# Sign of a converted weight set by a two-slope scaling on ScalarE instead of a second bit operation on VectorE, for 56 of the 68 weight pieces

## The chip, the cores and the metric

One Trainium2 chip; the kernel runs on one of its cores. The metric is the device time of one execution in microseconds (us). The engines are named as the profile names them: PE (TensorE matmul) and PEld (its weight load), DVE (VectorE), ACT (ScalarE), POOL (GpSimd), SP (SyncE).

## The reference, cut to what matters

A linear attention with exponential features, then two feed-forward layers:

```
q_p, k_p = phi(q * scale), phi(k * scale)      # exp(x @ omega.T - row maximum)
kv = einsum('bhsm,bhsd->bhmd', k_p, v)
x  = einsum('bhsm,bhmd->bhsd', q_p, kv) / den  # 2304 tokens x 512
xn = x / rms(x) * rms_g
y  = (silu(xn @ w_gate) * (xn @ w_val)) @ w_out        # hidden 1536
h  = y @ w_in
out = (h * cos(h)) @ w_out2                            # hidden 2048
```

The activations are float32, the five weight matrices reach the kernel as float64. The kernel has to turn each weight into float32 from its two 32-bit words before PE can use it, and it does so by arithmetic on their bits.

## The kernel before, in words

**Stages.** In the first stage (to about 311 us) PE works off 36 tiles of keys and queries (projection L392, transposes L410 and L468, sums L553 and L430) and, mixed into the later query tiles, the products of the first group of four of the twelve hidden columns of layer 1 (`product` L789, `out1` L854). The second stage (311 to about 586 us) does the other eight columns of layer 1 by seven products of half-size blocks (L1053, L1132). The third does layer 2 (L789 `h_ps`, L781 to L783 `o_ps`).

**The weights.** They are cut into 68 pieces of 128x512 values: 36 of layer 1 (for each of 12 columns f a gate piece e=0, a value piece e=1 and an output piece e=2) and 32 of layer 2 (16 columns, e=0 and 1). `Weights.todo` is their order: the twelve of the first group as gate, value, output of each column (so pieces 2, 5, 8 and 11 are output pieces), then for each of two groups of four columns the eight gate and value pieces and after them the four output pieces (20 to 23 and 32 to 35), then layer 2 (36 to 67).

**The conversion of one piece** is `exponent` and `front`:

- ACT (L161): the high words, read as float32 at a stride of two, are multiplied by 2**-112. That moves the exponent into place and gives W, of which there is one buffer.
- DVE (L167): f = W shifted left by 3, which drops the sign.
- DVE (L169): f = (W and SIGN) or f, which puts the sign back.
- DVE (L171): sign and exponent of f are written over the high words in `raw`.
- DVE (L178): the low words times 2**-52 times that, into `raw`.
- POOL (L183): f + that, the float32 value. `split` then makes a rounded high part (ACT, L188) and the rest (POOL, L191); pieces after the twelfth first go to DRAM (`keep`) and come back (`ask`).

**What sets the order.** Every engine takes its instructions in the order in which the program writes them. `front` is a generator with a yield after nearly every instruction; `tick`, `pace` and `get` take one step of it at fixed places between the attention's and the layers' own instructions. So the conversion's DVE operations stand in one queue with the row maxima (L401), the quotients (L440 to L442), the norm (L458), the transposed copies (L420), the gating (L840, L842) and the halves of x (L482), and W of the next piece (L161) stands in ACT's queue between the exponentials (L403), which PE's next products wait for. The ACT operation of piece c+1 is written after L171 of piece c.

The functions that the change touches, and what calls them:

Of the kernel before, what the change touches and what calls it, by code (L numbers as in the profile page):

```python
# [38 lines left out]
AF = mybir.ActivationFunctionType  # L39
ALU = mybir.AluOpType  # L40
# [8 lines left out]
SIGN = -(1 << 31)  # L49
# [6 lines left out]
def attention_then_ffn(ctx: ExitStack, tc: tile.TileContext, qT, kT, v, omT, wc1, rms_g, wc2, out, B, H, S, D):  # L56
    nc = tc.nc
# [50 lines left out]
    def f32(ap):  # L108
        return ap.bitcast(F32)
# [11 lines left out]
    class Weights:  # L121
# [26 lines left out]
        def load(self, c, queue=None):  # L148
            queue = queue or (nc.scalar if self.early else nc.sync)
            if c < len(self.todo) and c not in self.loaded:  # L150
# [4 lines left out]
                queue.dma_start(a, src.bitcast(I32).rearrange("p (n two) -> p n two", two=2))  # L155
                self.raw[c] = a

        def exponent(self, c):
            if c in self.raw:
                w = conv.tile([P, 512], I32, tag="W", name=f"W{c}", bufs=1)  # L160
                nc.scalar.mul(f32(w), f32(self.raw[c][:, :, 1]), 2.0 ** -112)  # L161
                self.w[c] = w

        def front(self, c):
            w, raw = self.w.pop(c), self.raw.pop(c)
            f = conv.tile([P, 512], I32, tag="f", name=f"f{c}", bufs=3)
            nc.vector.tensor_scalar(f, w, 3, None, op0=ALU.logical_shift_left)  # L167
            yield
            nc.vector.scalar_tensor_tensor(f, w, SIGN, f, op0=ALU.bitwise_and, op1=ALU.bitwise_or)  # L169
            yield  # L170
            nc.vector.tensor_scalar(raw[:, :, 1], f, SIGN_AND_EXPONENT, None, op0=ALU.bitwise_and)  # L171
            if not self.early:
                self.load(c + 2)
            yield
            self.exponent(c + 1)
            yield
            rest = f32(raw[:, :, 1])
            nc.vector.scalar_tensor_tensor(rest, raw[:, :, 0].bitcast(U32), 2.0 ** -52, rest,  # L178
                                           op0=ALU.mult, op1=ALU.mult)
            if c - 1 in self.f and c > self.fused:  # L180
                self.keep(c - 1)
            yield
            nc.gpsimd.tensor_tensor(f32(f), f32(f), rest, op=ALU.add)  # L183
            self.f[c] = f32(f)
            yield
# [325 lines left out]
    with tc.manual_schedule():  # L511
# [362 lines left out]
        def h_cos(blk, f, h, r, front, rate):  # L874
            o = fp.tile([P, 2, NB], F32R, tag="t", name=f"o{blk}_{f}", bufs=3)
            nc.scalar.activation(r, r, AF.Sin, bias=half_pi)  # L876
            wts.pace(front / 4, rate / 2)
            nc.vector.tensor_tensor(r, h, r, op=ALU.mult)  # L878
            nc.scalar.copy(o[:, 0], r)  # L879
            wts.pace(front / 4, rate / 2)  # L880
            nc.vector.tensor_tensor(o[:, 1], r, f32(o[:, 0]), op=ALU.subtract)  # L881
            return o
# [338 lines left out]
        for n in range(N2 + 2):  # L1221
            rate, front = 0, wts.rate(len(wts.todo) + 1, 52 - n)
            if n < N2:
                g = steps2[n][0]
                if n == starts[g] + 3:
                    wts.freed = base if g == 0 else done_at[g - 1]
                if g + 1 < len(GROUPS2) and n >= starts[g] + 3:
                    rate = rate_of(done_at[g + 1], starts[g + 1] - n - 8)
            if 2 <= n <= N2:
                hid[N1 + n - 1] = h_cos(*steps2[n - 1][1:3], *hid[N1 + n - 1], front, rate / 2)  # L1230
            flush(3)
            if due:
                unit()
                unit()
            for m in [n] if 0 < n < N2 - 3 else [n, n + 1] if n == N2 - 3 else [n + 1] if n == N2 - 2 else []:
                hid[N1 + m] = hidden(*steps2[m][1:3])
            if n >= 2:
                g0, b0, f0, st, en = steps2[n - 2]
                out2(g0, b0, f0, hid.pop(N1 + n - 2), st, en)
            if n in fetches:  # L1240
                fetch(fetches[n], f"yhl{steps2[n][0]}_{fetches[n]}")
            flush(3)
            if due:
                unit()
                unit()
            wts.pace(front / 2, rate / 2)
# [47 lines left out]
```

## Time and profile before

| | |
|---|---|
| three timed runs | 1000.8, 998.75, 999.22 us; median 999.22 |
| the profiled execution | 998.17 us, of which 996.4 us from the first instruction to the last |
| mean granted TensorE clock | 0.998 |
| PE, PEld | busy 977.5 us (98%), 922.8 us (93%) |
| DVE | busy 722.5 us (73%), 1251 instructions |
| ACT | busy 513.2 us (52%), 1117 instructions |
| POOL | busy 369.8 us (37%), 333 instructions |

PE's busy time is an average over three stages with different limits, so the table alone does not tell where PE waits; that is read from stretches. Busy times of PE come from modelled ends, and a busy PE can still be slower than its best. The chain of waits is the chain of work that ended last, followed back from the last instruction; "issue" in it is time in which an engine waited for nothing that the profile shows.

### The profile page before, as it was taken

To read this page: it belongs to the slowest core of one execution; us is meant where nothing else is said; L and a number is where in the kernel's file an instruction comes from. 1 tells how busy PE (TensorE), PEld (TensorE's weight loads), DVE (VectorE), ACT (ScalarE), POOL (GpSimd) and SP (SyncE) were. 2 spreads that over 40 slices of the span, in tenths; PEclk is the share of its full clock that TensorE was granted. 3 is DMA by queue.
4 is the path that set the end of the run, shared out by engine and by line. 5 is a ranking of instruction groups with operands and counts; after the bars stand their busy time and mean duration, and the time that the engine had idled before them with its cause. 6 is when DMAs were issued, how large, how long until landed. Compare 5 with 4: busy or idle time off the path is not lost.

```text
span 996.4 us, 16203 instructions
## 1 busy us (share of the span) xinstructions
PE 977.5 (98%) x5905; PEld 922.8 (93%) x5905; DVE 722.5 (73%) x1251; ACT 513.2 (52%) x1117; POOL 369.8 (37%) x333
## 2 busy tenths in 40 slices
PE   8999999998999999999999998999999999999998
PEld 7988998998999999999999997999999999999997
DVE  6797789988983558599776788776667776666655
ACT  6777775775533524346353545554444444434443
POOL 2133348747945866277433662111103310000000
PEclk9999999999999999999999999999999999999999
DMA  8555176785779788757978976443134442004201
GB/s 298 152 168 191 58 250 235 283 280 199 265 234 348 291 310 316 279 163 239 390 247 317 313 264 215 148 138 128 43 127 148 134 159 99 1 29 151 107 32 63
DMA packets 81438, 194.58 MB, mean 195 GB/s; under 512 B 8016, under 2 KB 38864, under 8 KB 81360
## 3 DMA queue, kind: packets, MB, share of 16 engines
q1 hardware_dynamic: 79920, 188.78, 54.2%
q10 hardware_dynamic: 1440, 4.78, 1.4%
q8 instruction: 46, 0.75, 0.3%
q14 instruction: 32, 0.26, 0.1%
HBM read 136.38 MB, written 57.15 MB: 194 GB/s over the span
## 4 chain that ended last, share of the span: by engine, by line
PE 84%; DVE 8%; issue 2%; ACT 2%; POOL 2%; ACTq 0%; DVEq 0%; POOLq 0%
PE h_ps L789 20%; PE X L1053 10%; PE y L1132 10%; PE Y L1053 8%; PE o_ps L783 7%; PE o_ps L782 7%; PE o_ps L781 6%; PE gv_ps L789 6%; PE y_ps L854 3%; PE kv_ps L553 2%; PE num_ps L430 2%; PE qp_ps L392 1%; DVE f L169 1%; PE kp_ps L392 1%; DVE f L167 1%
## 5 line engine op out<-in xcount | busy, mean ns | idle before, releaser
L789 PE MATMUL h_ps<-yhl,w 128*128 128x384 f32 x1152 | 217.2, 337 | 0.0
L789 PEld LDWEIGHTS h_ps<-yhl,w 128*128 128x128 f32 x1152 | 204.7, 188 | 8.1
L183 POOL TENSOR_TENSOR f<-f,raw 128x512 f32<-128x512 f32 x68 | 94.1, 1384 | 292.2 <-DVE raw L178 247.7
L191 POOL TENSOR_TENSOR w<-b,w 128x512 fp32r<-128x512 f32 x72 | 98.8, 1377 | 77.3 <-ACT w L188 67.7
L876 ACT ACTIVATE turns<-turns,half_pi 128x384 f32<-128x384 f32 x96 | 59.2, 617 | 110.4 <-DVE turns L871 110.4
L781 PE MATMUL o_ps<-w,o 128*128 128x512 f32 x288 | 112.1, 389 | 2.6 <-ACT o L879 2.6
L783 PE MATMUL o_ps<-w,o 128*128 128x512 f32 x288 | 114.0, 396 | 0.0
L782 PE MATMUL o_ps<-w,o 128*128 128x512 f32 x288 | 113.7, 395 | 0.0
L789 PE MATMUL gv_ps<-xhl,w 128*128 128x384 f32 x576 | 109.0, 337 | 1.8 <-DVE den L440 0.7
L789 PEld LDWEIGHTS gv_ps<-xhl,w 128*128 128x128 f32 x576 | 101.3, 189 | 3.2 <-issue 1.2
L1132 PE MATMUL y<-t,w 128*128 128x384 f32 x576 | 101.0, 334 | 0.0
L1132 PEld LDWEIGHTS y<-t,w 128*128 128x128 f32 x576 | 99.9, 188 | 0.0
L881 DVE TENSOR_TENSOR o<-turns,o 128x384 fp32r<-128x384 f32 x96 | 56.0, 583 | 50.0 <-ACT o L879 49.4
L879 ACT CAST o<-turns 128x384 fp32r<-128x384 f32 x96 | 49.3, 514 | 68.2 <-DVE turns L878 67.6
L878 DVE TENSOR_TENSOR turns<-h_ps,turns 128x384 f32<-128x384 f32 x96 | 53.4, 556 | 38.8 <-ACT turns L876 37.7
L1053 PE MATMUL X<-T,w 128*128 128x384 f32 x432 | 80.7, 334 | 0.0
L870 DVE SCALAR_TENSOR_TENSOR r<-turns,h_ps 128x384 f32<-128x384 int32 x96 | 53.1, 553 | 35.3 <-ACT turns L869 35.2
L1053 PEld LDWEIGHTS X<-T,w 128*128 128x128 f32 x432 | 75.4, 188 | 0.0
L869 ACT ACTIVATE turns<-h_ps,quarter 128x384 int32<-128x384 f32 x96 | 55.6, 580 | 32.2 <-PE h_ps L789 31.9
L783 PEld LDWEIGHTS o_ps<-w,o 128*128 128x128 f32 x288 | 54.0, 188 | 11.8 <-DVE o L881 0.3
L781 PEld LDWEIGHTS o_ps<-w,o 128*128 128x128 f32 x288 | 54.1, 188 | 11.6 <-ACT o L879 3.0
L169 DVE SCALAR_TENSOR_TENSOR f<-W,f 128x512 int32<-128x512 int32 x68 | 63.8, 939 | 1.0
(97 smaller groups left out, 1769.4 us busy)
## 6 DMA issues: line engine op xcount, KB each, us to landing
raw<-wc SPq DMA_DIRECT2D x59, 512.0 KB, 4.9
yhl<-yh_dram SPq DMA_DIRECT2D x32, 768.0 KB, 5.8
T<-T_dram SPq DMA_DIRECT2D x20, 768.0 KB, 9.2
kept<-f SPq DMA_DIRECT2D x56, 256.0 KB, 5.0
b<-kept SPq DMA_DIRECT2D x56, 256.0 KB, 4.1
B<-x_dram SPq DMA_DIRECT2D x15, 768.0 KB, 7.2
x_dram<-xhl SPq DMA_DIRECT2D x12, 768.0 KB, 5.8
s<-x_dram SPq DMA_DIRECT2D x24, 384.0 KB, 6.2
```

Source lines behind the costliest of these rows:

```text
L169: nc.vector.scalar_tensor_tensor(f, w, SIGN, f, op0=ALU.bitwise_and, op1=ALU.bitwise_or)
L183: nc.gpsimd.tensor_tensor(f32(f), f32(f), rest, op=ALU.add)
L191: nc.gpsimd.tensor_tensor(t[:, 1, to], src, f32(t[:, 0, to]), op=ALU.subtract)
L781: nc.tensor.matmul(o, w[0], x[0], start=first, stop=False)
L782: nc.tensor.matmul(o, w[0], x[1], start=False, stop=False)
L783: nc.tensor.matmul(o, w[1], x[0], start=False, stop=last)
L789: nc.tensor.matmul(o, w[i], x[j], start=n == 0, stop=n == len(terms) - 1)
L869: nc.scalar.activation(a, h, AF.Identity, bias=quarter, scale=1.0 / (2 * math.pi))
L876: nc.scalar.activation(r, r, AF.Sin, bias=half_pi)
L881: nc.vector.tensor_tensor(o[:, 1], r, f32(o[:, 0]), op=ALU.subtract)
L1053: nc.tensor.matmul(o, w[:, i, c + kk * P:c + (kk + 1) * P], x[:, j, kk], start=begin and n == 0, stop=n == 5, skip_group_check=True)
L1132: nc.tensor.matmul(acc[e], w[:, i, e * P:(e + 1) * P], t[:, j], start=f == fs[0] and i + j == 0, stop=f == fs[-1] and j == 1)
```

## The change: what it does

For 56 of the 68 pieces (all but the twelve output pieces of layer 1, which are layer 1, e=2) ACT's scaling becomes a parametric ReLU: a positive high word is multiplied by 2**-112 as before, a negative one by 2**-112 * 2**32. The exponent of a negative number so comes out larger by 32, and 32 in the exponent field is the bit that the shift by 3 moves into the sign's place. The DVE operation that put the sign back is not issued for these pieces; for the other twelve nothing changes.

```diff
+        def signed(self, c):
+            layer, f, e = self.todo[c]
+            return (layer, e) != (1, 2)
+
         def exponent(self, c):
             if c in self.raw:
                 w = conv.tile([P, 512], I32, tag="W", name=f"W{c}", bufs=1)
-                nc.scalar.mul(f32(w), f32(self.raw[c][:, :, 1]), 2.0 ** -112)
+                hi = f32(self.raw[c][:, :, 1])
+                if self.signed(c):
+                    nc.scalar.activation(f32(w), hi, AF.Prelu, scale=2.0 ** -112, alpha=2.0 ** 32)
+                else:
+                    nc.scalar.mul(f32(w), hi, 2.0 ** -112)
                 self.w[c] = w
...
             nc.vector.tensor_scalar(f, w, 3, None, op0=ALU.logical_shift_left)
             yield
-            nc.vector.scalar_tensor_tensor(f, w, SIGN, f, op0=ALU.bitwise_and, op1=ALU.bitwise_or)
+            if not self.signed(c):
+                nc.vector.scalar_tensor_tensor(f, w, SIGN, f, op0=ALU.bitwise_and, op1=ALU.bitwise_or)
             yield
```

The yields stay, so no other instruction changes its place: PE, ACT, POOL and SP have the same instructions in the same order as before, ACT's loads of activation tables among them (26 before, 26 now), and DVE has 1197 rows in place of 1253. The change adds nine lines above, so L161 becomes L167 (two-slope) or L169 (plain), L167 becomes L175, L169 becomes L178, L171 becomes L180, L178 becomes L187.

DVE's queue around the conversion of piece 26 (f26, W26, raw26; the stretch at about 257 us), before. The reductions over qmx17 are row maxima of the last query tile, y3 is an output row, xhl5 a half of x:

```order
L401 TENSOR_REDUCE qmx17_1_3295<-qp_ps17_1_3278 128x4
L167 TENSOR_SCALAR f26_3310<-W26_3226 128x512
L169 SCALAR_TENSOR_TENSOR f26_3310<-W26_3226,f26_3310 128x512
L171 TENSOR_SCALAR raw26_3127<-f26_3310 128x512
L178 SCALAR_TENSOR_TENSOR raw26_3127<-raw26_3127 128x512
L818 COPY y3_1_3370<-y_ps0_3_0_1_2969 128x384
L482 TENSOR_TENSOR xhl5_0_3338<-xT_ps15_3333,xhl5_0_3338 128x2x128
```

The same place with the change:

```order
L410 TENSOR_REDUCE qmx17_1_3277<-qp_ps17_1_3260 128x4
L175 TENSOR_SCALAR f26_3292<-W26_3208 128x512
L180 TENSOR_SCALAR raw26_3110<-f26_3292 128x512
L187 SCALAR_TENSOR_TENSOR raw26_3110<-raw26_3110 128x512
L827 COPY y3_1_3351<-y_ps0_3_0_1_2953 128x384
L491 TENSOR_TENSOR xhl5_0_3319<-xT_ps15_3314,xhl5_0_3319 128x2x128
```

One instruction is gone and those behind it move up; W26 has its last reader one instruction earlier.

ACT's queue where the first products of layer 1 set in (at about 97 us), before; qe5 and qe6 are exponentials of query tiles, gv0 the first SiLU:

```order
L161 ACTIVATE W9_1242<-raw9_1096 128x512
L403 ACTIVATE qe5_0_1256<-qp_ps5_0_1246,qmx5_0_1257 128x128 x4
L403 ACTIVATE qe5_1_1263<-qp_ps5_1_1247,qmx5_1_1264 128x128 x4
L188 CAST w8_1313<-f8_1190 128x512
L155 DMA raw11_1315<-wc1 128x1024
L835 ACT_TABLE_LOAD
L835 ACTIVATE gv0_0_1334<-gv_ps0_0_0_1321 128x384
L449 ACTIVATE sq4_1336,ms4_1337<-x4_1281 128x512
L161 ACTIVATE W10_1342<-raw10_1194 128x512
```

The same place with the change, where W9 and W10 are the two-slope form:

```order
L167 ACTIVATE W9_1236<-raw9_1091 128x512
L412 ACTIVATE qe5_0_1250<-qp_ps5_0_1240,qmx5_0_1251 128x128 x4
L412 ACTIVATE qe5_1_1257<-qp_ps5_1_1241,qmx5_1_1258 128x128 x4
L197 CAST w8_1307<-f8_1184 128x512
L155 DMA raw11_1309<-wc1 128x1024
L844 ACT_TABLE_LOAD
L844 ACTIVATE gv0_0_1328<-gv_ps0_0_0_1315 128x384
L458 ACTIVATE sq4_1330,ms4_1331<-x4_1275 128x512
L167 ACTIVATE W10_1335<-raw10_1188 128x512
```

Nothing moved here: the two-slope form stands among exponentials as well as behind a SiLU, and no load of a table stands ahead of it.

## Rows read from the trace of the kernel before

**Rows 1.** Busy time by stretch: stretch, its us; busy us (instructions) per engine; clock; DMA.
```profile
4.30:49.40 45.10, 43.73 (x449) 40.65 (x450) 33.63 (x62) 34.28 (x116) 9.79 (x9) 1.00 0.70 230
49.40:108.60 59.20, 55.31 (x502) 50.48 (x503) 48.59 (x96) 45.96 (x136) 21.16 (x21) 1.00 0.49 161
108.60:225.00 116.40, 114.47 (x834) 110.58 (x833) 99.43 (x189) 81.39 (x181) 69.17 (x70) 1.00 0.68 235
225.00:284.00 59.00, 54.96 (x348) 52.51 (x347) 52.47 (x84) 28.11 (x64) 47.41 (x48) 0.97 0.66 224
284.00:586.00 302.00, 302.00 (x1744) 302.00 (x1743) 209.25 (x322) 135.71 (x283) 171.91 (x142) 1.00 0.82 291
586.00:606.00 20.00, 17.35 (x92) 15.91 (x91) 14.99 (x26) 9.54 (x18) 6.71 (x5) 1.00 0.74 246
606.00:990.00 384.00, 384.00 (x1926) 347.76 (x1925) 261.17 (x463) 176.72 (x319) 42.78 (x31) 1.00 0.29 103
```

**Rows 2.** L169 alone: DVE busy us (instructions) up to 311 us and after.
```profile
0.00:311.00 311.00, 31.58 (x32) 0.99 0.66 225
311.00:996.00 685.00, 32.26 (x36) 1.00 0.51 182
```

**Rows 3.** L169 as a line: duration ns min/median/max, first and last start us.
```profile
L169 DVE SCALAR_TENSOR_TENSOR f<-W,f x68: 675/692/1720, 12.3 to 784.5; 128x512 int32<-128x512 int32 x68
```

**Rows 4.** The chain of waits to 284 us, pieces of L169: start us, us, what.
```profile
12.27 0.70 DVE f L169
...
15.59 0.04 DVE f L169
15.63 1.54 issue
...
54.33 0.61 DVE f L169
...
81.56 0.61 DVE f L169
...
95.39 1.68 DVE f L169
...
125.54 0.70 DVE f L169
...
134.96 0.70 DVE f L169
...
225.54 1.40 DVE f L169
...
247.40 1.06 DVE f L169
...
257.51 1.39 DVE f L169
...
265.05 1.38 DVE f L169
```

**Rows 5.** POOL in order of time beside the L169 that starts at 257.51 us.
```profile
256.19 2.16 POOL L590 TENSOR_TENSOR s<-s,s 128x384 f32<-128x384 f32 x2
```

**Rows 6.** PE in order of time: its longest idle time in the first stage.
```profile
236.72 1.16 PE L392 MATMUL qp_ps<-om,qraw 64*128 64x128 f32 x14 [2.39 <-DVE xhl L482]
```

**Rows 7.** Busy time by stretch around that idle time, as rows 1.
```profile
235.00:240.00 5.00, 3.29 (x21) 3.17 (x22) 4.86 (x12) 1.23 (x5) 4.67 (x8) 0.80 0.12 43
240.00:245.00 5.00, 5.00 (x26) 5.00 (x26) 3.52 (x6) 3.89 (x11) 1.04 (x1) 0.86 0.93 298
```

**Rows 8.** ACT's groups: line op, tiles, count; busy us, mean ns; idle before.
```profile
L161 ACT ACTIVATE W<-raw 128x512 f32<-128x512 f32 x68 | 46.8, 688 | 24.2 <-DVE f L169 13.8 <-issue 3.6 <-DMA y<-y_dram 2.8
...
L876 ACT ACTIVATE turns<-turns,half_pi 128x384 f32<-128x384 f32 x96 | 59.2, 617 | 110.4 <-DVE turns L871 110.4
...
L1058 ACT ACTIVATE r<-r 128x384 f32<-128x384 f32 x48 | 25.1, 527 | 40.5 <-DVE r L1088 32.5 <-DVE r L1081 7.9
...
L835 ACT ACT_TABLE_LOAD x13 | 16.7, 1283 | 0.2
```

## The prediction

> **What bounds the kernel now.** I read the busy times by stretch first, since the mean over the span (PE 98%) hides where PE waits. From 284 to 586 us and from 606 to 990 us PE is busy in every microsecond [rows 1]: there nothing that VectorE saves can be seen. PE is idle in the four stretches up to 284 us: 45.10 - 43.73 = 1.37, 59.20 - 55.31 = 3.89, 116.40 - 114.47 = 1.93 and 59.00 - 54.96 = 4.04 us, together 11.2 us, and for 20.00 - 17.35 = 2.65 us at the change to layer 2, at 586 to 606 us [rows 1]. In the second, third and fourth stretch DVE is the fullest engine after PE (48.59 of 59.20, 99.43 of 116.40 and 52.47 of 59.00 us), and the reader is to see that 52.47 of 59 leaves it hardly a gap in which to be late without someone waiting.
>
> Then the chain of waits, which says whether the removed operation itself stands on the path. It does: in the first 284 us the chain goes eleven times through L169 [rows 4]. By the order of the pieces these are 0, 1, 4, 7, 9, 12, 13, 23, 25, 26 and 27. Only piece 23 (at 225.54 us) is an output piece and keeps its operation. Last, the line itself and POOL beside it: L169 takes 0.69 us in the median but up to 1.72 [rows 3].
>
> **What is removed.** 56 of 68 operations. 32 of the 68 run before 311 us and cost 31.58 us [rows 2]. Of those 32 pieces eight are output pieces (2, 5, 8, 11, 20 to 23), so 24 go, some 24/32 of 31.58 = 23.7 us of DVE time. The other 32 removed operations lie behind 311 us under a PE that never stops, apart from the change to layer 2, where one L169 runs at about 600 us; I count all of these at nothing. Their cover is PE's own work; were it gone, they would be worth at most 32.26 us [rows 2].
>
> What the 24 are worth has to be told from the chain, since DVE time is worth nothing where PE or ACT is waited for instead. Taken with their whole length on the chain the ten removed ones are 0.70 + 1.58 (0.04 and the 1.54 of issue behind it) + 0.61 + 0.61 + 1.68 + 0.70 + 0.70 + 1.06 + 1.39 + 1.38 = 10.4 us [rows 4].
>
> That is too much, because the long ones are collisions. The L169 at 257.51 us takes 1.39 us, and all of it runs beside two POOL additions that last from 256.19 to 258.35 us [rows 4, 5]; without such company it is 0.70 [rows 4]. If DVE's next operation (L171) meets the same POOL addition in its place, only 0.69 us is won. The Trainium skill has the rule for this ("Advanced Engine Details and Errata", section VectorE Performance Modes: the second SBUF port of VectorE is shared with GpSimd, so that such instructions block each other); by it the stall is POOL's and is handed on, without it all 10.4 us would come back. The trace agrees with a stall, and no row before the change shows the handing on. I take 0.69 for each long one, by the median of the line [rows 3]:
>
> - to 49 us, pieces 0 and 1: 0.70 + 0.69 = 1.4, but PE is idle for only 1.37 us there, part of it before 11 us: **1.0**
> - 49 to 109 us, pieces 4, 7 and 9: 0.61 + 0.61 + 0.69 = 1.9; pieces 5 and 8, which keep theirs, stand in between, so that a part is waited away again: **1.6** of 3.89 us idle
> - 109 to 225 us, pieces 12 and 13: 0.70 + 0.70: **1.4** of 1.93
> - 225 to 284 us, pieces 25, 26 and 27: 3 x 0.69: **2.1** of 4.04. The longest single idle time, 2.39 us at 234 to 237 us [rows 6], lies behind piece 23 and behind additions on the pieces of layer 1, and I leave it as it is.
>
> Sum 6.1 us.
>
> **What is added.** On ACT the scaling gets a slope for negative numbers, an immediate like the scale. Its price is not in the trace. The nearest row below is the same line without it (688 ns, so +0); a gain is excluded, since the tile and the stride are the same. The nearest above is what a second operand costs: a 128x384 function with a pointer as bias takes 617 ns, one without 527 [rows 8], so +90 ns. I take 0, since scale and slope are both immediates, and keep 0.09 us for the range: 24 of them are 2.2 us on ACT, which is busy for 28.11 to 81.39 us of these stretches [rows 1] and so can take most of it aside. W (one buffer) comes free one operation earlier, at the end of the shift; ACT, which waits for that in its queue with exponentials behind it, can only start sooner. I cost that at nothing.
>
> **Moved.** Nothing but what follows from time: the raw pieces are asked for behind L171, the stores behind L178, on SP's queue in the same order, some 0.7 us earlier each. POOL's addition L183 waits for L178 and comes as much sooner.
>
> Against the profiled execution that is 998.17 - 6.1 = 992.1 us. That execution lies 1.05 us under the median of the three runs (999.22), and a new median should lie as far above its own profile: **993.1 us**.
>
> **The clock.** One more term has no sure sign. Behind the idle time of 2.39 us the granted clock falls to 0.80 and 0.86 in two stretches of 5 us [rows 6, 7]: 5 x 0.20 + 5 x 0.14 = 1.7 us of PE time at the full level. If the pieces before it bring DVE there earlier, this can vanish; another wait of that length elsewhere would cost as much. It is 0 in the sum and 1.7 us in the range.
>
> **Rivals.**
>
> *All of the idle time comes back.* DVE was late everywhere, the stalls with POOL vanish with the operation and are not handed on: 10.4 us by the chain, at most the 11.2 us that PE is idle; 999.22 - 11.2 = 988.0 us, 986.3 if the clock stays up too. For it: DVE's 52.47 of 59 us. Against: PE is idle behind ACT and behind output pieces too. Chance 0.12.
>
> *Hidden anyway.* The chain counts each step as if nothing else were due. If behind L169 the exponentials on ACT or POOL's addition are due just as late, only the last stretch gives something, and there one piece in two: some 1 us, with the start 1.7 us; 997.5 us. For it: between 109 and 225 us PE is busy 98% although DVE is at 85% [rows 1]. Against: piece 25 to 27 within 18 us on the chain. Chance 0.18, half of it within what can be told from no change.
>
> *Slower: the two-slope form needs a table of its own.* Then each of the 24 pieces would cost a load and the next exponential or SiLU another: 2 x 1.283 = 2.57 us [rows 8]. In the first two stretches ACT is busy 34.28 + 45.96 = 80.2 of 104.3 us [rows 1], and eight pieces would add 20.5 us: ACT would be full, and with half of that on the path PE would lose 10 us, against 6.1 won: some 1003 us. It decides from the point where a piece costs ACT more than the 0.69 us that DVE gets back. The Trainium skill warns of just that ("ScalarE: Activation LUTs", section Table sets: the hidden batching unit: a function outside the active set costs a table load); the trace has such loads, at 1283 ns as the page says. Against: the listing of ACT's instructions has the same 26 loads at the same places. Chance 0.04, the case counted in that collisions fall worse than before.
>
> *The change doesn't do what it says*: a slope that is not applied would cost the same time, so this has no price of its own.
>
> **How the numbers follow.** My forecast, a gain of 3.5 to 9 us, has 0.66. A measurement of this kernel can tell some 0.2%, 2 us, from no change. Faster by more than that: 0.66 + 0.12 + half of 0.18, less a little = 0.86; within it 0.10; slower 0.04. The range leaves out the cases within 2 us of no change and the slower ones (0.14) and some of the largest gains: from 999.22 - 2.0 = 997.2 down to 999.22 - 11.2 - 1.7 = 986.3, which I put at 986.5.
>
> **What would show it right.** L169's successor with 12 instructions, eight of them before 311 us; DVE busy less by 56 times 0.7 us up to the mean of 63.84 / 68 = 0.94 us [rows 2], 39 to 53 us; the two-slope form at 688 ns within 0.09; PE idle to 284 us down from 11.2 to some 5 us; the chain without the ten places; no change between 311 and 990 us but an earlier start. Collisions that are handed on would show as a successor of L171 with a longer mean than L171 had. It would be wrong if the ACT operation took longer by 0.1 us or more, if a table load stood beside it, or if PE's idle time moved behind ACT or POOL at the same length.

## The result, and the profile after

The changed kernel takes 991.01 us in the median of five runs (989.46 to 991.8), the kernel before 998.81 (five runs, 997.83 to 1000.8): a ratio of 0.9918 with a 95% interval of [0.9903, 0.9932], 7.8 us. The profiled execution of the change took 991.8 us with a span of 990.0 us; it is the longest of the five, while the profiled execution before, 998.17 us, lies below its median. By the two profiles the gain is therefore 6.4 us, and by the medians 7.8.

The page of the change, busy time by engine:

```profile
PE 976.8 (99%) x5905; PEld 923.6 (93%) x5905; DVE 674.1 (68%) x1195; ACT 512.1 (52%) x1117; POOL 361.7 (37%) x333
```

DVE has 56 instructions fewer and 48.4 us less to do (722.5 before), 0.86 us for each. POOL, which nothing was taken from, has 8.1 us less (369.8 before).

Groups of instructions of the change (line, engine, operation, tiles, count; busy us, mean ns; idle before):

```profile
L187 DVE SCALAR_TENSOR_TENSOR raw<-raw 128x512 f32<-128x512 uint32 x68 | 57.8, 850 | 0.4
L175 DVE TENSOR_SCALAR f<-W 128x512 int32<-128x512 int32 x68 | 42.8, 629 | 7.2 <-ACT W L167 5.5 <-ACT W L169 1.6
L180 DVE TENSOR_SCALAR raw<-f 128x512 int32<-128x512 int32 x68 | 42.2, 620 | 0.7
L167 ACT ACTIVATE W<-raw 128x512 f32<-128x512 f32 x56 | 38.5, 687 | 7.6 <-DVE f L175 5.7 <-DMA raw<-wc 1.9
L844 ACT ACT_TABLE_LOAD x13 | 16.7, 1283 | 0.2
L178 DVE SCALAR_TENSOR_TENSOR f<-W,f 128x512 int32<-128x512 int32 x12 | 10.5, 876 | 0.1
L200 POOL TENSOR_TENSOR w<-b,w 128x512 fp32r<-128x512 f32 x72 | 95.2, 1327 | 80.6 <-ACT w L197 71.3 <-DVE t L851 7.6 <-PE y L1141 1.6
```

The same three neighbours in the kernel before:

```profile
L178 DVE SCALAR_TENSOR_TENSOR raw<-raw 128x512 f32<-128x512 uint32 x68 | 54.3, 799 | 0.4
L171 DVE TENSOR_SCALAR raw<-f 128x512 int32<-128x512 int32 x68 | 41.6, 612 | 1.3
L191 POOL TENSOR_TENSOR w<-b,w 128x512 fp32r<-128x512 f32 x72 | 98.8, 1377 | 77.3 <-ACT w L188 67.7 <-DVE t L842 5.5 <-DMA raw<-wc 2.3
```

The two-slope form takes 687 ns, the plain one 688 [rows 8]. DVE's next operations became longer on the mean of all 68 (L178's 799 ns is L187's 850, L171's 612 is L180's 620), and POOL's subtractions that make the rests of the rounded weights became shorter (L191's 1377 is L200's 1327).

Busy time of the change in the stretches of [rows 1]:

```profile
4.30:49.40 45.10, 44.97 (x460) 41.90 (x460) 31.89 (x62) 34.54 (x119) 9.98 (x9) 1.00 0.74 236
49.40:108.60 59.20, 56.86 (x514) 52.22 (x513) 44.45 (x93) 47.03 (x141) 21.02 (x21) 1.00 0.51 157
108.60:225.00 116.40, 115.74 (x844) 111.90 (x843) 94.43 (x182) 79.53 (x178) 71.20 (x75) 1.00 0.69 240
225.00:284.00 59.00, 56.58 (x361) 55.63 (x361) 48.30 (x85) 31.60 (x73) 46.62 (x48) 0.97 0.72 251
...
590.00:595.00 5.00, 2.35 (x8) 1.45 (x8) 3.94 (x8) 1.99 (x4) 0.73 (x1) 0.88 1.05 327
595.00:600.00 5.00, 5.00 (x22) 4.44 (x21) 3.39 (x6) 2.54 (x6) 0.71 (x1) 0.77 0.53 193
```

PE is idle to 284 us for 0.13 + 2.34 + 0.66 + 2.42 = 5.55 us (11.2 before). The last two lines are stretches at the change to layer 2, and what they show is new: the granted clock is 0.88 and 0.77 there, where before all of 586 to 606 us had 1.00 [rows 1]. By 5 x 0.12 + 5 x 0.23 that is an estimated 1.75 us of PE time.

The chain of waits of the change, its conversion pieces to 284 us that answer to [rows 4], and the start of the second stage (start us, us, what):

```profile
63.74 0.68 ACT W L167
...
92.45 1.43 DVE raw L180
...
219.59 0.73 DVE f L175
220.35 1.40 DVE f L178
...
303.26 2.08 PE X L1062 x12
```

Of the eleven places where the sign's operation stood on the chain, one is left: 220.35 is piece 23, an output piece. 92.45 is piece 9, where the sign's operation stood for 1.68 us [rows 4], beside a POOL addition (L183, 95.10 to 96.51 us). Now L180 stands there beside the same addition, with 1.43 us where L171 took 0.43: the collision was handed to the next operation. The second stage starts at 303.26 us. Before:

```profile
311.16 2.08 PE X L1053 x12
```

That is 7.9 us earlier. Compared at the same matmul (the n-th of PE, its start in either trace), the change is ahead by 1.3 us at 49.4 us of the trace before, by 2.9 at 108.6, 5.2 at 225, 7.9 at 284 and still 7.9 at 585; at 606 it is ahead by 6.4, and so to the end. So the gain of the stretches is 1.3, 1.6, 2.3 and 2.7 us, and 1.5 us are given back between 585 and 606. Only 5.7 us of the 7.9 are idle time of PE that went away (11.2 to 5.55); the other 2.2 come from time in which PE counts as busy. For the same 2294 matmuls up to the second stage it is busy for 298.70 us before and 296.48 in the change, with a clock of 0.99 in both: idle time is no upper bound of the gain here.

Idle times of PE in the change (start us, us, what; in brackets the idle time and who ended it):

```profile
231.53 1.65 PE L401 MATMUL qp_ps<-om,qraw 64*128 64x128 f32 x14 [2.42 <-DVE xhl L491]
...
592.98 0.50 PE L790 MATMUL o_ps<-w,o 128*128 128x512 f32 x1 [2.65 <-ACT o L888]
```

The first is the 2.39 us of [rows 6], as long as before. The second was 2.65 us before too; only the clock behind it is new.

### The profile page after: what moved, and what is told of

It reads as the page before. It is cut to its first block, busy times and chain, and to the rows that moved or that the text cites. A ratio compares the mean times of both kernels' runs of the same rounds, so it can differ in the third digit from the quotient of the medians.

```text
span 990.0 us, 16129 instructions
## 1 busy us (share of the span) xinstructions
PE 976.8 (99%) x5905; PEld 923.6 (93%) x5905; DVE 674.1 (68%) x1195; ACT 512.1 (52%) x1117; POOL 361.7 (37%) x333
## 4 chain that ended last, share of the span: by engine, by line
PE 89%; DVE 4%; POOL 2%; DMA 2%; issue 2%; ACT 2%; SPq 0%; ACTq 0%; DVEq 0%; POOLq 0%
PE h_ps L798 20%; PE X L1062 10%; PE y L1141 10%; PE Y L1062 8%; PE gv_ps L798 7%; PE o_ps L792 7%; PE o_ps L791 7%; PE o_ps L790 7%; PE y_ps L863 4%; PE kv_ps L562 4%; PE num_ps L439 2%; PE kp_ps L401 2%; PE qp_ps L401 2%; PE eT_ps L419 1%; DMA x_dram<-xhl 1%
## 5 line engine op out<-in xcount | busy, mean ns | idle before, releaser
L200 POOL TENSOR_TENSOR w<-b,w 128x512 fp32r<-128x512 f32 x72 | 95.2, 1327 | 80.6 <-ACT w L197 71.3
L880 DVE SCALAR_TENSOR_TENSOR turns<-turns,r 128x384 f32<-128x384 int32 x96 | 61.6, 641 | 3.3
```

What stands on the lines that cost most here:

```text
L200: nc.gpsimd.tensor_tensor(t[:, 1, to], src, f32(t[:, 0, to]), op=ALU.subtract)
L880: nc.vector.scalar_tensor_tensor(f32(a), a, -TWO_PI_LO, b, op0=ALU.mult, op1=ALU.add)
```

## The experiments

Each ratio is against the kernel before, run beside it on the same chip (medians of 998.16 us for runs 1 to 4, 998.78 for 5 to 8, 998.0 for 9 and 10). The ratios with their intervals are estimates of their own and differ from the quotients of the medians by up to 0.0008. Theory: VectorE's queue is late in the first stage, and all of the gain is its freed time there. The rivals: the part on ScalarE costs or gives something; or the gain comes from where the pieces of layer 2 are.

**1. Only the 24 pieces of the first stage.**

```diff
-            return (layer, e) != (1, 2)
+            return (layer, e) != (1, 2) and c < 36
```

> Two slopes and no second bit operation for the 24 pieces before 311 us alone; the 32 pieces of layer 2 as before. Theory A (all of the gain is DVE time in the first stage): PE reaches the second stage some 7.9 us earlier than before, as with the whole change, and the time is lower by 6.4 to 8.2 us. Theory B (a good part of the gain is in layer 2, behind 311 us): under 5 us. On the second fall of the clock at the change to layer 2, which the profile of the change has and that of before has not: if it comes from the layer 2 pieces' missing operations, it is gone here and the whole 7.9 us stays; if it comes from when the same 2.65 us of idle time falls, it can be there or not.

991.5 us in the median, ratio 0.9927 [0.9913, 0.9942]. The second stage starts at 303.15 us, 8.0 us earlier than before. Within the intervals this is the whole change. To the same matmul DVE is busy for 226.6 us in place of 249.9 before: 23.4 us for 24 operations, 0.97 each, and the sign's operation took 0.99 on the mean of this stage (31.58 / 32 [rows 2]). So VectorE got nearly all of the operations' time back. The clock falls at 593 us here as well, so the operations that are missing in layer 2 are not what makes it fall.

**2. Only the 32 pieces of layer 2.**

```diff
-            return (layer, e) != (1, 2)
+            return layer == 2
```

> The reverse: the change for the 32 pieces of layer 2 alone. Theory A: no difference before 311 us, and within 1 us at the end (up to 1.7 us slower if the clock falls at the change to layer 2). Theory B: faster by 3 us or more.

998.03 us, 0.9999 [0.9990, 1.0008]: nothing. The 0.6 us by which its trace is ahead stand there from its first microseconds, before any piece differs; so much the start varies between profiled executions.

**3. The slope, and VectorE's operation kept** (56 pieces get the two slopes, all 68 keep the operation, which then sets a bit that is set).

```diff
-            if not self.signed(c):
-                nc.vector.scalar_tensor_tensor(f, w, SIGN, f, op0=ALU.bitwise_and, op1=ALU.bitwise_or)
+            nc.vector.scalar_tensor_tensor(f, w, SIGN, f, op0=ALU.bitwise_and, op1=ALU.bitwise_or)
```

> The two-slope form on ACT for the 56 pieces, and the bit operation on DVE kept for all 68 (it then sets a sign that is set already). It prices ACT's part alone. Theory A (a second immediate costs nothing): the ACT operation at 688 ns within 10 ns and the time within 1 us of before. Rival (the slope costs ACT like a second operand, 90 ns, and the exponentials behind it wait): slower by 1 to 3 us.

998.39 us, 0.9999 [0.9991, 1.0008]. Its groups:

```profile
L167 ACT ACTIVATE W<-raw 128x512 f32<-128x512 f32 x56 | 38.4, 686 | 23.4 <-DMA y<-y_dram 8.5 <-DVE f L177 8.2 <-issue 3.6
...
L177 DVE SCALAR_TENSOR_TENSOR f<-W,f 128x512 int32<-128x512 int32 x68 | 62.9, 926 | 1.0
```

The slope is free: 686 ns, and no time lost.

**4. Neither slope nor operation.** The 56 pieces are scaled plainly (by 2**-113 in place of 2**-112), so the sign of these weights is left out.

```diff
-                    nc.scalar.activation(f32(w), hi, AF.Prelu, scale=2.0 ** -112, alpha=2.0 ** 32)
+                    nc.scalar.mul(f32(w), hi, 2.0 ** -113)
```

> The bit operation on DVE left out for the 56 pieces, with ACT's scaling in the plain form: the sign of these weights is left out, and they are scaled by 2**-113 in place of 2**-112 on the high word. It prices DVE's part alone. Theory A: the same as the whole change, 6.4 to 8.2 us faster than before. Rival (the two-slope form costs something that the gain hides): faster than the whole change by 1 to 3 us.

991.25 us, 0.9924 [0.9909, 0.9939], as the change (0.9918 [0.9903, 0.9932]). Runs 3 and 4 together: the gain belongs to VectorE's missing operation, and the slope neither adds nor takes. They don't separate two ways in which the operation can act, its time in VectorE's queue and its hold on W, which ACT waits for: in the kernel before ACT waits 7.8 us in five places to 311 us until the sign's operation lets W go, in run 3 again 7.8 us in five, and in the change 1.5 us in two until the shift does. How much of the gain came this way is open.

**5 and 6. Eight pieces of one stretch alone**: pieces 12 to 19 (`return 12 <= c < 20`) and pieces 24 to 31, as here:

```diff
-            return (layer, e) != (1, 2)
+            return 24 <= c < 32
```

> The change for pieces 12 to 19 alone (converted between 124 and 195 us). Theory A (each stretch gives its own share): PE reaches the second stage 1.4 us (the term of the prediction) to 2.3 us (what the whole change gave between 109 and 225 us) earlier than before. Rival (the shares hang together: a stretch gives only what DVE has been relieved of before it): under 0.7 us.

> The change for pieces 24 to 31 alone (239 to 295 us). Theory A: 2.1 us (the term of the prediction) to 2.7 us (what the whole change gave between 225 and 284 us). If collisions with POOL were not handed on, 3.8 us, the length that pieces 25 to 27 had on the chain. Rival (shares hang together): under 1 us.

Pieces 12 to 19: 997.78 us, 0.9989 [0.9980, 0.9998]; at the start of the second stage 2.3 us ahead, of which 1.5 go at 590 to 606 us with the clock. Pieces 24 to 31: 996.31 us, 0.9973 [0.9962, 0.9983]; 2.6 us ahead, and the clock stays up at the change to layer 2. In the change the same stretches give 2.3 and 2.7 us, so the parts add up, and what DVE gets back in one stretch is not lost in the next.

In the first of the two, 1.5 of the 2.3 us come between 146 and 172 us. The chain of the kernel before holds L169 only for 0.04 us there, and much of POOL:

```profile
153.67 1.73 POOL f L183
...
158.30 1.01 POOL ms L454
...
162.71 1.44 DVE f L167
```

The chain of the run with pieces 12 to 19:

```profile
152.85 1.28 POOL f L192
...
157.52 0.56 POOL ms L463
...
161.48 0.28 DVE f L175
```

Two of POOL's operations are shorter by 0.45 us each, and the chain ran through them. The first (1.73 to 1.28 us) began while the sign's operation of piece 15 ran beside it; the second (1.01 to 0.56) lost the company of L178, which now ends before it. But PE's own waits show more than the chain: 1.3 of the 1.5 us are one idle time of PE in the kernel before, behind the halves of x (L482) that stand in VectorE's queue right behind the sign's operation of piece 15:

```profile
152.89 1.37 DVE L169 SCALAR_TENSOR_TENSOR f<-W,f 128x512 int32<-128x512 int32 x1
```

```profile
154.97 1.16 PE L392 MATMUL qp_ps<-om,qraw 64*128 64x128 f32 x16 [1.25 <-DVE xhl L482]
```

With pieces 12 to 19 changed, the halves of x follow on the shift and that idle time is gone. VectorE's queue and POOL's additions both came earlier; no run separates their shares.

**7. The operation twice for the 24 pieces** of the first stage, in the kernel before.

```diff
             nc.vector.scalar_tensor_tensor(f, w, SIGN, f, op0=ALU.bitwise_and, op1=ALU.bitwise_or)
+            layer, _, e = self.todo[c]
+            if (layer, e) != (1, 2) and c < 36:
+                nc.vector.scalar_tensor_tensor(f, w, SIGN, f, op0=ALU.bitwise_and, op1=ALU.bitwise_or)
```

> The kernel before with the bit operation issued twice for the 24 pieces before 311 us. Theory A (DVE stands on the path all along that stage, so the operation is worth as much added as taken away): slower by 7 to 12 us, 0.7 to 1.2%. Rival (what the change took away was just a surplus, and one more finds its place beside PE or costs more because nothing is left): under 4 us or over 15 us.

1011.64 us, 1.013 [1.0115, 1.0145], with DVE busy for 738.9 us (+16.4, 0.68 for each of 24). Its page, the group of the added operation, and the start of its second stage:

```profile
PE 983.5 (97%) x5905; PEld 927.3 (92%) x5905; DVE 738.9 (73%) x1275; ACT 513.3 (51%) x1117; POOL 372.2 (37%) x333
```

```profile
L172 DVE SCALAR_TENSOR_TENSOR f<-W,f 128x512 int32<-128x512 int32 x24 | 21.6, 899 | 0.8
```

```profile
324.05 2.08 PE X L1056 x12
```

12.9 us late: more than taking one away gives, and a little more than the 12 us that were expected at most. 3.4 us of it are a clock of 0.57 granted from 159 to 167 us (8 x 0.43), a new fall; the other 9.5 are 0.4 us for each operation, against 7.9 / 24 = 0.33 for taking one away. (The other three executions have a mean clock of 0.995, the profiled one 0.993, so they lost less of it.) POOL is busy for 372.2 us, 2.4 more than before, with the same instructions. VectorE's time in this stage is on the path in both directions.

**8. The four output pieces 20 to 23 as well** (60 pieces), which stand before the idle time of 2.4 us that the change left.

```diff
-            return (layer, e) != (1, 2)
+            return (layer, e) != (1, 2) or 20 <= c < 24
```

> The whole change and in addition the four output pieces 20 to 23 (197 to 227 us), 60 pieces in all. Piece 23 is the one operation that the chain of the changed kernel still shows (1.40 us at 220 us), ahead of PE's longest idle time of 2.4 us. Theory A: another 0.7 to 1.4 us before 243 us, and if the idle time falls under the point at which the clock falls there, 1.7 us more: faster than before by 7 to 11 us. Rival (the 2.4 us belong to the additions on the pieces of layer 1, which run beside POOL): the same as the change within 0.5 us at 243 us.

988.43 us, 0.9900 [0.9884, 0.9917]. The idle time, and the stretch around it:

```profile
229.62 1.16 PE L401 MATMUL qp_ps<-om,qraw 64*128 64x128 f32 x14 [1.50 <-DVE xhl L491]
```

```profile
228.00:234.00 6.00, 4.50 (x35) 4.26 (x34) 5.86 (x13) 2.32 (x9) 5.75 (x8) 1.00 0.30 109
234.00:240.00 6.00, 6.00 (x41) 5.96 (x40) 3.90 (x8) 5.95 (x13) 4.31 (x6) 1.00 0.94 282
```

The same stretches of the change:

```profile
228.00:234.00 6.00, 3.58 (x26) 3.05 (x25) 5.86 (x13) 1.51 (x3) 5.75 (x8) 0.84 0.30 109
234.00:240.00 6.00, 6.00 (x33) 6.00 (x32) 3.89 (x7) 4.87 (x14) 1.49 (x2) 0.88 0.82 263
```

The idle time goes from 2.42 to 1.50 us and the clock stays at 1.00 behind it, which is worth an estimated 6 x 0.16 + 6 x 0.12 = 1.7 us. At the start of the second stage the run is 11.2 us ahead of the kernel before, 3.3 more than the change. So 0.9 us of that idle time did hang on the output pieces' operations before it. That the shorter wait is what kept the clock up is likely and not shown: in run 4's profile it stayed up behind 2.41 us too.

**9. The last step before layer 2 on POOL**: the subtractions for the last block, in `add_y`, which DVE makes ahead of the products of layer 2.

```diff
-            at(2, lower, t, a, nc.vector)
+            at(2, lower, t, a, nc.gpsimd if blk == 1 else nc.vector)
```

> The whole change, and the four subtractions that make the low halves of the last block of y (at 585 to 590 us) on POOL in place of DVE. In the change PE is idle for 2.65 us there behind DVE's queue, and the clock falls right behind it (1.5 us lost by 606 us). Theory (the fall follows the idle time and has nothing to do with the change itself): with some 2.8 us less in DVE's queue PE's idle time goes to under 1 us, the fall goes with it, and the time is 3 to 4.3 us under that of the change: 10 to 12 us faster than before. Rival (POOL or the DMA that brings y holds the place): within 1 us of the change.

990.4 us, 0.9916 [0.9901, 0.9931], no different from the change: the 10 to 12 us of the theory did not come, and the time is the one that the rival had. The idle time at layer 2 is shorter:

```profile
591.98 0.50 PE L790 MATMUL o_ps<-w,o 128*128 128x512 f32 x1 [1.02 <-ACT o L888]
...
593.20 0.50 PE L792 MATMUL o_ps<-w,o 128*128 128x512 f32 x1 [0.49 <-DVE o L890]
```

No fall of the clock follows it, and the 1.5 us that the change gives back there stay. But in the profile the fall at 230 us is longer and costs 6 x 0.31 + 6 x 0.26 = 3.4 us, where the change lost 1.7, although nothing differs from the change up to there:

```profile
228.00:234.00 6.00, 3.60 (x21) 3.19 (x21) 5.58 (x13) 1.15 (x4) 5.67 (x9) 0.69 0.29 106
234.00:240.00 6.00, 6.00 (x28) 6.00 (x27) 2.73 (x5) 3.95 (x12) 1.03 (x1) 0.74 0.88 296
```

The one of its five executions that had a mean clock of 0.999 (the others 0.996 or 0.997) took 987.37 us.

**10. Both, 8 and 9.** The edits are those two.

> The same four subtractions on POOL, together with two slopes for the output pieces 20 to 23 as well (60 pieces). Theory: the two add up, 10.3 us of the 60 pieces and 3 to 4.3 us: 13 to 15 us faster than before. Rival: as the 60 pieces alone, 10 us.

987.25 us, 0.9889 [0.9875, 0.9902], the fastest of all and below the change's interval. In the profiled execution (985.72 us) PE has its full clock throughout; the two places are:

```profile
228.71 1.16 PE L401 MATMUL qp_ps<-om,qraw 64*128 64x128 f32 x14 [1.49 <-DVE xhl L491]
...
587.19 0.50 PE L790 MATMUL o_ps<-w,o 128*128 128x512 f32 x1 [1.01 <-ACT o L888]
```

In the profile the gain is 998.17 - 985.72 = 12.5 us, in the medians 10.8. The other three executions have a mean clock of 0.998 and take 987.23 to 988.04 us; where in them it fell was not recorded. So the two edits don't quite add up in the medians: run 8 had 998.78 - 988.43 = 10.4 us, and the 1.5 us at layer 2 bring it to 10.8 only, nearer the rival's 10 than the 13 to 15 of the theory.

## Why the prediction was right, point by point

The forecast of 993.1 us was 2.1 us too high; direction, stage and engine held. That the sum came so near is in part luck. The first stage gave 7.9 us where the sum has 6.1, and 1.5 of these 1.8 us were lost again to a fall of the clock that the sum does not have. Its four terms were right for their stretches to 0.9 us, and less so for the places in them.

**What bounds the kernel: right.** All of the gain lies in the first stage (run 1 against run 2), and it is VectorE's operation that gives it (runs 3 and 4).

**To 49 us, taken as 1.0: measured 1.3, and 1.5 without the start.** At the matmul that starts at 12.04 us before, ahead of the first of the sign's operations (12.27), the change is 0.2 us behind; from there to 49.4 us it gains 1.5. The five other runs with these pieces (1, 4, 8, 9, 10) gain 1.5 there too, from starts that differ by 0.8 us. The chain's 0.70 + 0.69 was nearly right, and the cut to 1.0 for PE's idle time was not.

**49 to 109 us, taken as 1.6: measured 1.6, by luck.** The step was 0.61 + 0.61 + 0.69 less a little. By the same matmul 1.1 us come between 62 and 64 us (behind piece 4), 0.5 between 84 and 88 (behind piece 7), and nothing between 90 and 109, where piece 9 has its 0.69. At piece 4 a second collision left VectorE as well: L171 right behind the sign's operation took 1.38 us before, L180 there takes 0.42, and POOL's instruction beside it takes 1.78 in place of 1.38. At piece 9 the collision went to L180 (1.43 us, above), and what VectorE had saved it then waited for ACT's SiLU (2.20 us idle in place of 1.48).

**109 to 225 us, taken as 1.4: measured 2.3, and for another reason.** The step was "pieces 12 and 13: 0.70 + 0.70". The run with pieces 12 to 19 gives only 0.3 us between 108.6 and 146 us, where those two stand (behind piece 13; behind piece 12 nothing), and 1.5 us between 146 and 172, most of it PE's idle time of 1.25 us behind piece 15, where the chain held POOL's additions. The chain is one path, the one that ended last; a wait of PE beside it is not on it, and a step on it can have another right behind it that is due as late.

**225 to 284 us, taken as 3 x 0.69 = 2.1: measured 2.7** in the change and 2.6 alone (run 6). The step was that each long collision gives 0.69 and hands the rest on to L171. By the same matmul 0.9 us come behind piece 25, 0.1 behind piece 26, 0.8 behind piece 27, and 0.9 between 280 and 284 us, behind pieces 28 and 29, for which the prediction has nothing. The handing on is there at single places (piece 9: L171's 0.43 us is L180's 1.43), and over all 68 pieces mainly one operation further, at L178's successor (+51 ns each, 3.5 us in all). But other DVE groups became shorter by as much, and the reading that only 0.69 of a long collision comes back did not hold in sum: in this stage VectorE got back 0.97 us per operation (run 1), nearly the 0.99 that L169 took there. What falls short is what PE gets of it, a third. The prediction also has the L169 at 257.51 us run beside two POOL additions for all of its 1.39 us; these end at 258.35, and the last 0.55 us run beside a cast. The trace shows the conflict on both sides: POOL too got faster, by 8.1 us of 369.8. The rule of the Trainium skill ("Advanced Engine Details and Errata", section GPSIMD Details: GpSimd shares a read and a write interface with VectorE and conflicts with VectorE instructions in a two-port mode or with two inputs from SBUF) agrees with that, since the sign's operation has two such inputs, W and f. The rule does not say how much of a stall is handed on.

**The price on ACT, taken as 0: right.** 687 ns against 688, and run 3 at 0.9999. The slower rival, a table of its own for the two-slope form, fell with it: ACT's 13 loads of 1283 ns [rows 8] are 13 at 1283 ns (L844 of the change), and ACT is busy for 512.1 us against 513.2.

**W's earlier release, taken as nothing: not shown.** ACT's waits for it fell from 7.8 to 1.5 us in the first stage, and no run takes the operation's time away without its hold on W.

**"Hidden anyway" and "all of the idle time comes back": neither as a whole.** Pieces 9 and 12 gave nothing, as the first of these rivals has it for most pieces. PE's idle time to 284 us went to 5.55 us where I had written "some 5". Part of what is left belongs to the output pieces, and run 8 shows it: 2.42 us to 1.50. The 11.2 us that I put as the most were no bound: run 8 is 11.2 us ahead at 284 us, 1.7 of them by the clock, with 4.6 us of idle time left.

**Layer 2 at nothing: right** (run 2).

**The clock, 0 with 1.7 to either side: the size held, the place didn't.** I looked at the fall behind [rows 6], which stayed. The fall that cost 1.5 us is new and stands at the change to layer 2, behind idle time that was there before. That it costs time in the timed runs as well can be read from their mean clocks: four executions of the change with 0.996 took 990.58 to 991.8 us, the one with 0.998 took 989.46. Why it falls there is open. It is not that operations are missing in layer 2: run 1 has all of these, and the fall.

**The median from the profile.** I wrote 998.17 - 6.1 = 992.1 us for a profiled execution, and 991.8 came. The step to the median, "should lie as far above its own profile", had the wrong sign: the profile of the change lies 0.8 us above its median. The 1.05 us came from three runs; of 23 later runs of the kernel before the median is 998.16, as its profile. The step (1.05 + 0.8) and 0.3 us of the sum are the 2.1.

## What to carry to other kernels

Where an engine's queue is nearly full in a stretch in which PE idles, an operation less on it was worth a third of its time here (0.33 of 0.97 us). The chain of waits told the stage and not the places: two of its steps gave nothing, and the largest single gain, 1.3 us, stood beside it. Read PE's own idle times with the chain, look at what the next operation will run into, and at what runs beside it on an engine that it blocks. A choice by sign went into a two-slope scaling that another engine makes anyway, at no cost in its duration here. After such a change, look for the clock behind the idle times that are left: one that was harmless before can cost 1.5 us.

## What the runs showed of the hardware that was not expected

- **Collisions cost both engines.** With 56 operations less on DVE, POOL's same 333 instructions took 8.1 us less. With the slope and the operation kept (run 3) they took 370.9 us, with neither (run 4) 361.7, so it is the operation and not the slope. Single ones went from 1.73 to 1.28 us and from 1.01 to 0.56 (run 5).
- **The same idle time of PE is followed by half clock in some profiled executions and not in others.** At the change to layer 2, PE is idle for 2.64 to 2.66 us in the kernel before, in the change and in runs 1 to 8; the clock fell behind it in the change and in runs 1, 4, 5, 7 and 8, and not in the kernel before and in runs 2, 3 and 6. With 1.0 us in place of it (runs 9 and 10) it did not fall in the profiles. At about 230 us it fell behind 2.4 us in nine profiles of ten, and behind 1.5 us (runs 8 and 10) in neither. What decides between equal idle times is open; there is one profile of each program here, and run 9's longer fall at 230 us stands where its instructions are still those of the change.
- **The first microseconds vary between profiled executions.** At the matmul that starts at 12.04 us in the kernel before, ahead of any effect of the edits, the others lie between 0.2 us behind and 0.7 us ahead, up to a tenth of this change's worth.
